# Eight single PSUM banks and one-bank FFN jobs for the first unit in a fused block-sparse attention and gated FFN kernel, under a newly written task order

## The chip, the cores and the metric

The kernel runs on one core of one Trainium2 chip. The metric is the device time of one execution in microseconds (us). The trace comes from one further, profiled execution; its span goes from the first instruction of the core to the last.

## The reference, cut to what matters

```python
# q, k, v: (4, 8, 768, 64) f32; sampled_blocks: (24, 3); blocks of 32 tokens
scores = (q @ k.T) / 8
mask = band of blocks (|i - j| <= 1) | first and last block row and column
mask |= the 3 sampled key blocks of each query block
attn = softmax(where(mask, scores, -1e9))
x = (attn @ v).transpose(0, 2, 1, 3).reshape(3072, 512)
out = (sigmoid(x @ w_gate) * (x @ w_val)) @ w_out   # 512 -> 1536 -> 512, f32 out
```

The mask is the same for all batches and heads. The kernel computes the full 768x768 scores of each head and multiplies the exponentials by the 0/1 mask (for the first unit a bias is added to the scores instead).

## The kernel before, in words

**Units.** The work is cut into 12 units: unit n is a batch b = n // 3 and 256 of its 768 queries. A unit has four pairs of heads. For a pair there are three score steps: TensorE multiplies the transposed q and k (`qT`, `kT`) into a PSUM slot of two banks, ScalarE (ACT) takes the exponential into an f16 tile `P` (L586, 128x1024), and VectorE (DVE) multiplies it by the mask (L592). In unit 0 there is no multiplication: a matmul of `bias` and `e` adds the mask to the scores. Then `value` multiplies `P` by `vex` (v with a column of ones), DVE normalises it (L655 reciprocal, L656 product) into `x`, and `x` is transposed into `xT`. For units 0 and 1, `value` uses all 128 rows of TensorE and `xT` is made by TensorE transposes (L467); for later units `value` runs as two alternating row tiles of 64, DVE folds the two halves (L646), and `xT` is made by a transposing DMA on SP's queue (L706).

**FFN.** Units 0 to 3 are FFN groups by themselves, the other eight form four groups of two. A job `f` of a group multiplies `xT` by two 128-column tiles of w_gate and w_val for one unit, or by one for two units, into a slot of two banks; ACT takes the tanh (L801) of 128x512 values, DVE makes `ht` with it (L804). Then `y` multiplies `ht` by w_out; ACT (L886) or DVE (L888) brings the result to `ysb`, and SP stores it (L878). All matmuls of scores, values and FFN are issued at one helper line, L352, so in the profile they are told apart by their tiles: `m<-qT,kT` are scores, `m<-xT,wg` FFN. TensorE is in one of two kinds of mode: whole (128 rows) or in row tiles of 64.

**PSUM.** The 16 KB of each partition are four units of two banks, `m0` to `m3`. Every task that needs PSUM takes one of the four, however little it writes, until ACT or DVE has read it.

**Inputs of batch 0.** k and q of the first pair come as f32 through SP and ACT; the other q, k, v and all weights through GpSimd (POOL) DMAs that convert to f16, in the order of `FIRST`: k1 q1 k2 q2 k3 q3 v0 v1 v2 v3 r0 w0 r1 w1 r2 w2 r3 w3 w4 w5 o0 o1 o2. Here r0 to r3 are the remaining q rows of the four pairs, w0 to w5 pairs of column blocks of w_gate and w_val, o0 to o2 w_out. q and k of batch 0 are transposed by TensorE (L467, L472) in 64-row quarters, and ACT or DVE copies them out (L297, L299). For batches 1 to 3, POOL loads a pair (L226), DVE repacks it (`pair_up`, L525, into `kp` or `qp`, one buffer for each pair), and SP issues a transposing DMA into `kT` or `qT` (L536). v is copied into `vex` by DVE (L545).

**The order.** All tasks are numbered as the program makes them. The table `ORDER` (L40 to L99) lists them in the order in which their instructions are issued. A token `123D:2@45` is task 123, on DVE, with PSUM slot 2, its load held until task 45. `Plan.run` (L137) walks through it. Each engine executes its own instructions in that order, so an instruction that waits holds up all behind it on its engine. `jN` tokens are junk matmuls that raise TensorE's clock at the start. The planner's other fields (durations, lags) are of no effect at run time.

Of the kernel before, what the change touches and what calls it, by code (L numbers as in the profile page):

```python
# [22 lines left out]
NT = S // 128  # L23
# [8 lines left out]
PE, ACT, DVE, DMA, SP = "PADGS"  # L32
# [4 lines left out]
EARLY = 2  # L37
# [3 lines left out]
j3 j3 j3 j3 j3 j3 j3 j3 5A 8D j3 0 11A j3s 9:0 j3s j3s j3s 10D j3s j3s 12:1 1:2 j3s 13A 3:0 2 j3s 34:1 4D 35 15:2  # L41
j3s 32:3 16D 6:0 33 17:1 7D 117:2 18D 97:0 118D 44:1 98A j3s 22:3 78:2 23D 45 36:0 79D 20:3 37 21D
40:2 25:1 30:3 41 26D 76:0 77D 46:1 31 54:2 19 74:0 47 75D 27:3 24 55 50:0 28D 80:1 64:3 51 81D
48:2 65 60:1 49 56:0 61 14 66:3 58:2 67D 105@30 57 29 89:3 59 38:1 90 52:0 86:2 53D 87 39 68:3
93:0 69D 62:1 108:2 94 42:3 109 43D 102:0 63D 111:3 70:1 103 110 126:2 71D 112 104 95:0 84:1 96D
122:3 85A 113 140:0 127 123 91 130:1 128 132:3 141 129 131 72:2 119:0 99:1 73D 133 120 147:2 134
100 135 142 157:0 148 154:3 171:1 124 155 149 158 88 164:3 143:2 156 176:0 92@164 144 121 146@111
101 172 170@44 165 173 161:2 217@54 145 190:1 177 189@46 162 125@40 178 237@54 159 186:3 191 150:2
115:0 151D 192 174:2 187 116 204:1 175 188 231:0 179:3 183:2 232 205 180D 244:3 184 233 206 166
245 82:0 200:2 218 83D 201 246 234:3 193:0 219 194A 152 235 185 153 211:2 136:0 220 137D 212 138  # L50
272:3 195 139 229 223A 202 167:0 255:2 168 236 273 213 221A 239 214:0 230 307:1 274 169 215 275
256 240 216 197:3 308 257 196 181 198 258 248:0 309 182 199 241:2 249 242 310 268:3 262 225:1 250
260 114@268 263 269 251 252:2 226 318:0 261 207:3 319 253 315:1 208 289:2 316 160@315 254 106:0
265:3 243 290 107A 247@265 266 270 276:1 209 291 300:0 293:3 277 301 278 282:1 294 292 283 297 163
303:0 335:2 295 302 222 304 279 227 285:1 336 296 286 238 359:0 305 337 360 210 284 331:3 228
362:1 348 332 361 264 349 363 333 328:0 287 350 329 267 322:3 351A 320 344:1 353A 311:0 323
203@344 345 341:2 387:3 321@359 312 342 317 271@282 426:1 373:0 313 411@300 427 330 397:2 374 398
343 388 346 375 259 408:1 376 389 355:2 400@268 409 390 347@30 419:0 356 334@89 380:3 405:1 428
370:2 381 306@111 364 420 288@44 406 371 386@214 366:3 421 410 365@265 454:2 422 433:1 455 432@380
# [3 lines left out]
442 474:1 484:0 463A 378 465A 339 467:2 452 340 475 524:3 480 485 525 514 354 515:1 327 468 486  # L63
# [4 lines left out]
538 583 438 550:1 567 571 542 439 586 551 638:0 563:2 572 425 539 564 552 595:1 573A 404 577:2 604  # L68
639 574 596 578 609:0 568 597 555 575A 627:2 598 616:3 610 628 617 543@616 635:1 565 712@200 630:2
611 569@300 636 612 592:3 446@563 688:0 631 593 658@60 689 654 706:1 556@231 588:3 707 579 641@550  # L70
640 642:0 632 676@471 619:1 633 589 587@282 620 594 691@214 623:2 690 613 590 670:1 591 643 671
637 605:3 624 644 621 606 645 659:1 618 625 709:0 681:3 710 626 660 607 655:2 682 692:0 656 453
663:3 711 726@99 661 657 608@234 673:2 693 662 674 622@652 664 672 694 548 699:1 695 665 723:2 666
# [3 lines left out]
762 669 782 730:3 745A 734:0 760 757:2 731 735 753 798:3 703 758 799 732 736 764:0 759 750 743A  # L77
600 765 797 826:3 823:1 767 763 824 650 816:0 766 651 827 809:1 756 768 810 719 800 787:3 817 769
733 788 806:1 801:0 807 770D 819:3 789 772A 811 737:1 790:2 839 738 614 802 580 615 791 803 601
# [5 lines left out]
904 856 925 936:0 978:1 913 937 911 857 919:3 979 908 875:0 920 914 876 929:1 921 917A 905 932  # L85
970:3 930 935 971 877 922 946:0 915A 1024:3 931 947 893 1025 928 1027:2 1012:0 939 938 916 1013
948 959:3 1028 966 1040:0 940 960 1041 1026 941 967:2 973:3 944A 942D 968 945 1029 952:0 1001:1
# [6 lines left out]
1078 1074 1094 1008 1082 1095 1083 1084 1100:1 1087A 1096A 1108:3 1088 1098A 1101 1085A 1099 1097  # L94
# [19 lines left out]

class Bank:


    def __init__(self):
        self.slot = None


class Plan:

# [13 lines left out]
    def run(self):  # L137
        done = set()
        for token in self.order:
            if token[0] == "j":  # L140
                self.idle(int(token[1]), token[2:])
                continue
# [1015 lines left out]
```

## Time and profile before

| | us |
|---|---|
| runs, as timed | 278.1, 278.46, 278.68 |
| median of the runs | 278.46 |
| the profiled execution's own time (its span) | 277.8 |
| TensorE busy | 270.0 |
| DVE busy | 207.1 |
| ACT busy | 192.1 |
| POOL (issue of DMAs) busy | 47.3 |
| granted TensorE clock | 0.999 of full |

A row of a view by windows gives the window, its length, and then for each engine the busy time and the number of instructions, the granted clock, the share of DMA engines and GB/s. A row of a timeline gives start, duration, engine, line and tiles; in brackets stands how long the engine stood idle before and what released it. The chain of waits is followed back from the last instruction: start, duration, and what the time went to. A matmul's listed duration includes the way through the pipeline; what it costs TensorE is the distance to the next start. The same holds on DVE and ACT to a smaller degree.

### The profile page before, as it was taken

How to read it: one execution, taken by the hardware profiler on the slowest of the kernel's cores; microseconds unless marked ns; L12 is line 12 of the kernel's file. 1: busy time of each engine (PE TensorE's matmuls, PEld its weight loads, DVE VectorE, ACT ScalarE, POOL GpSimd, SP SyncE). 2: the span in 40 equal slices, each digit the busy share in tenths (PEclk: the TensorE clock that was granted, in tenths of full speed). 3: DMA queues.
4: the chain of work that ended last, by engine and by line, in shares of the span. 5: the costliest groups of instructions: out<-in, count | busy, mean ns of one | idle time of the engine just before them, and what ended most of it. 6: DMA issues, size and time to landing. Idle time of an engine off the chain costs nothing.

```text
span 277.8 us, 11169 instructions
## 1 busy us (share of the span) xinstructions
PE 270.0 (97%) x5007; PEld 178.7 (64%) x5007; DVE 207.1 (75%) x421; ACT 192.1 (69%) x243; POOL 47.3 (17%) x69
## 2 busy tenths in 40 slices
PE   8879999999999999999999999999999999999995
PEld 3667785896897798655566655655655676555543
DVE  4667788899999989978988886887876899004422
ACT  3988868899989958968868965679688571035300
POOL 7776261030480000028300000000000000000000
PEclk9999999999999999999999999999999999999999
DMA  7999999994599693339986743014130002230004
GB/s 160 175 195 197 200 205 198 140 139 100 84 160 145 117 140 97 103 98 167 142 113 113 73 61 97 2 21 142 24 96 4 4 2 76 70 151 2 0 2 151
DMA packets 56684, 28.93 MB, mean 104 GB/s; under 512 B 33036, under 2 KB 53692, under 8 KB 56636
## 3 DMA queue, kind: packets, MB, share of 16 engines
q0 software_dynamic: 21520, 13.90, 35.7%
q1 hardware_dynamic: 34628, 14.02, 24.8%
q8 instruction: 39, 0.64, 1.0%
q10 hardware_dynamic: 488, 0.30, 0.3%
q14 instruction: 9, 0.07, 0.1%
HBM read 28.47 MB, written 6.29 MB: 125 GB/s over the span
## 4 chain that ended last, share of the span: by engine, by line
PE 87%; DMA 7%; POOL 2%; ACT 1%; DVE 1%; issue 1%; SPq 0%
PE m L352 86%; DMA q<-in_q_dram 3%; DMA v<-in_v_dram 2%; DMA kT<-kp 1%; ACT P L586 1%; POOL k L226 1%; POOL q L226 1%; POOL wg L236 0%; POOL wv L236 0%; DVE ysb L888 0%; DVE P L592 0%; ACT ysb L886 0%; PE m L472 0%; PE m L467 0%; ACT ysb L929 0%
## 5 line engine op out<-in xcount | busy, mean ns | idle before, releaser
L586 ACT ACTIVATE P<-m 128x1024 f16<-128x1024 f32 x144 | 143.1, 1025 | 27.8 <-PE m L352 24.6
L352 PE MATMUL m<-xT,wg 64*128 64x512 f16 (+2 forms) x720 | 136.7, 326 | 0.1
L352 PE MATMUL m<-xT,wv 64*128 64x512 f16 (+2 forms) x720 | 136.7, 326 | 0.0
L592 DVE TENSOR_TENSOR P<-P,mask 128x1024 f16<-128x1024 f16 x132 | 87.0, 684 | 2.7 <-ACT P L586 2.6
L352 PEld LDWEIGHTS <-wg 64*128 64x128 f16 (+1 forms) x720 | 66.6, 94 | 21.2 <-issue 0.8
L352 PEld LDWEIGHTS <-wv 64*128 64x128 f16 (+1 forms) x720 | 66.4, 94 | 18.2 <-issue 0.5
L804 DVE SCALAR_TENSOR_TENSOR ht<-th,m 128x512 f16<-128x512 f32 x72 | 49.0, 685 | 37.0 <-ACT th L801 36.1
L352 PE MATMUL m<-wo,ht 64*128 64x512 f16 (+2 forms) x564 | 70.4, 372 | 0.0
L801 ACT ACTIVATE th<-m 128x512 f32<-128x512 f32 x72 | 42.8, 598 | 29.6 <-PE m L352 26.1
L352 PE MATMUL m<-qT,kT 64*128 64x256 f16 x576 | 53.6, 269 | 0.9 <-DMA kT<-kp 0.5
L352 PEld LDWEIGHTS <-P 64*128 64x128 f16 (+1 forms) x2112 | 41.1, 94 | 5.2 <-issue 0.4
L352 PEld LDWEIGHTS <-ht 64*128 64x128 f16 (+1 forms) x564 | 29.4, 94 | 23.4 <-issue 1.3
L352 PE MATMUL m<-vex,P 64*128 64x65 f16 (+1 forms) x2112 | 42.5, 190 | 0.0
L352 PEld LDWEIGHTS <-kT 64*128 64x128 f16 x576 | 26.7, 94 | 17.8 <-issue 1.3
L646 DVE TENSOR_REDUCE acc<-m 128x260 f32<-128x520 f32 x40 | 27.8, 697 | 7.9 <-PE m L352 6.8
L226 POOL DMA_DIRECT2D k<-in_k_dram x15 | 11.1, 744 | 48.3 <-PE m L352 45.0
L886 ACT ACTIVATE ysb<-m 128x512 f32<-128x512 f32 x18 | 10.2, 601 | 11.8 <-PE m L352 11.8
L656 DVE TENSOR_TENSOR x<-acc,rz 128x256 f16<-128x256 f32 x40 | 17.0, 425 | 1.4
L226 POOL DMA_DIRECT2D v<-in_v_dram x16 | 11.6, 736 | 33.5 <-PE m L352 12.9
L226 POOL DMA_DIRECT2D q<-in_q_dram x19 | 13.9, 733 | 3.9 <-DMA wo<-in_moe_w_out_dram 1.8
L352 PE MATMUL m<-bias,e 64*128 64x256 f16 x48 | 5.9, 271 | 2.3 <-DVE mask L299 1.9
L929 ACT ACTIVATE ysb<-m 128x256 f32<-128x256 f32 x1 | 0.4, 383 | 10.1 <-PE m L352 10.1
(47 smaller groups left out, 84.1 us busy)
## 6 DMA issues: line engine op xcount, KB each, us to landing
out_dram<-ysb SPq DMA_DIRECT2D x23, 256.0 KB, 2.4
v<-in_v_dram POOLq DMA_DIRECT2D x16, 192.0 KB, 5.1
k<-in_k_dram POOLq DMA_DIRECT2D x15, 192.0 KB, 6.6
q<-in_q_dram POOLq DMA_DIRECT2D x12, 192.0 KB, 6.4
wg<-in_moe_w_gate_dram POOLq DMA_DIRECT2D x6, 256.0 KB, 8.4
wv<-in_moe_w_val_dram POOLq DMA_DIRECT2D x6, 256.0 KB, 9.0
wo<-in_moe_w_out_dram POOLq DMA_DIRECT2D x3, 512.0 KB, 12.8
xT<-x SPq DMA_TRANSPOSE x40, 2.4
```

Of the source, the lines that this page charges most:

```text
L226: return nc.gpsimd.dma_start(dst[:, h0:h1, t0:t1, :], src[b, h0:h1].rearrange("h (p t) d -> p h t d", t=NT)[:, :, t0:t1, :],)
L352: return nc.tensor.matmul(out, lhsT, rhs, start=start, stop=stop, skip_group_check=True).ins
L586: nc.scalar.activation(self.pt.rearrange("a h i n -> a (h i n)"), both(self.bank).rearrange("a h n -> a (h n)"), AF.Exp, bias=0.0, scale=SCALE
L592: nc.vector.tensor_tensor(self.pt, self.pt, m.unsqueeze(1).broadcast_to([128, 2, 2, UQ]), op=ALU.mult,)
L646: nc.vector.tensor_reduce(self.acc.rearrange("a h s d -> a (h s d)"), self.parts.rearrange("a r n -> a n r"), axis=mybir.AxisListType.X, o ...
L656: nc.vector.tensor_tensor(self.x16.rearrange("a s h d -> a h s d"), self.acc[:, :, :, 0:D], rz.broadcast_to([128, 2, 2, D]), op=ALU.mult,)
L801: nc.scalar.activation(th, both(bank)[:, 0, :], AF.Tanh, bias=0.0, scale=0.5)
L804: nc.vector.scalar_tensor_tensor(self.ht[:, tiles[0] : tiles[-1] + 1, :], in0=th.rearrange("a (f n) -> a f n", n=self.w), scalar=1.0, in1= ...
L886: nc.scalar.activation(ysb, both(bank)[:, s, :], AF.Copy, bias=0.0, scale=0.5)
L929: nc.scalar.activation(ysb, src, AF.Copy, bias=0.0, scale=0.5)
```

## The change: single banks, and a new order

PSUM becomes one tile `m` of eight banks. A task may take a two-bank slot (0 to 3) as before, or a single bank (a to h).

```diff
+    @property
+    def single(self):
+        return self.slot in "abcdefgh"
...
-    units_ps = [ps.tile([128, 2, 512], f32, name=f"m{i}") for i in range(4)]
+    banks = ps.tile([128, 8, 512], f32, name="m")
+    units_ps = [banks[:, 2 * i : 2 * i + 2, :] for i in range(4)]
...
+    def one(bank):
+        i = "abcdefgh".index(bank.slot)
+        return units_ps[i // 2][:, i % 2, :]
```

In a single bank a mask tile's two halves (`mask_tiles`) both use the same 64 rows and so run one after the other. Transposes go as whole 128-row transposes of 128x128, or of 128x64 for q and k, and not as four 64-row quarters. `value` of units 0 and 1 and the last outputs (`y_last`) use one bank.

```diff
-    def halves(out16, tiles):
+    def turned_in(bank, tiles):
...
+            flat = len(tile_.shape) == 2
+            if bank.single:
+                if flat:
+                    nc.tensor.transpose(one16(bank)[:, i * 128 : (i + 1) * 128], tile_, ident)
+                    continue
```

With `SMALL = 1`, unit 0's FFN is 12 jobs `f1` of one bank in place of 6 jobs `f` of two. Each has eight matmuls of 128x256, a tanh and a product of 256 columns. The first four (before: the first two) are split, so that the last quarter of the sum can come later.

```diff
-EARLY = 2
+EARLY, SMALL = 4, 1
...
+        def f1(self, f):
+
+            bank = Bank()
+            i = len(used["th1"])
+            th = home("th1", i)
...
+                                one(bank)[:, g * UQ : (g + 1) * UQ],
+                                (wg, wv)[g][:, c, f * 128 : (f + 1) * 128],
+                                self.x[:, c, :],
...
+            if self.g < SMALL:
+                for f in range(self.per * j, self.per * (j + 1)):
+                    self.f1(f)
+                return
```

The repacking `pair_up` of a pair is also made to depend on the transposing DMA that read its buffer in the batch before:

```diff
-            a = pair_up(nm, *((k16, kp) if nm == "k" else (q16, qp)), b, p, [ld] + old)
+            a = pair_up(nm, *((k16, kp) if nm == "k" else (q16, qp)), b, p, [ld] + old + turned_b.get((nm, p), []))
...
+            turned_b[nm, p] = [c]
```

`FIRST`, the tiles in SBUF, the groups and the DMAs are as they were. `ORDER` is new from the first token; TensorE's order of tasks agrees again from the second part of group 4's outputs on (161 tasks of TensorE, at about 158 us in the trace before). Its first lines:

```diff
-j3 j3 j3 j3 j3 j3 j3 j3 5A 8D j3 0 11A j3s 9:0 j3s j3s j3s 10D j3s j3s 12:1 1:2 j3s 13A 3:0 2 j3s 34:1 4D 35 15:2
+11A 8 j3 j3 j3 j3 j3 j3 j3 j3 j3 9Q:a 0 j3s 1:b 2 5 12:1 10A 3:2 4 13A j3s 34:0 6:1 7 15:3 16 82:2
```

Of its many moves, three places follow. The first is TensorE's queue where the second part of q's third pair (r2, tile `q_79`) is transposed. Before, it stands directly behind scores of unit 1:

```order
L352 MATMUL m_132<-qT_86,kT_88 128x256
L352 LDWEIGHTS kT_88
L352 MATMUL m_132<-qT_86,kT_88 128x256
L352 LDWEIGHTS kT_88
L352 MATMUL m_132<-qT_86,kT_88 128x256
L472 LDWEIGHTS q_79
L472 MATMUL m_130<-const,q_79 64x64
```

Behind the 16 transposes the first FFN job of unit 0 begins there (`m_131<-xT_159,wg`). In the changed kernel:

```order
L365 MATMUL m<-xT_156,wg 128x256
L365 LDWEIGHTS wv
L365 MATMUL m<-xT_156,wv 128x256
L365 LDWEIGHTS wg
L365 MATMUL m<-xT_156,wg 128x256
L365 LDWEIGHTS wv
L365 MATMUL m<-xT_156,wv 128x256
L501 LDWEIGHTS q_79
L501 MATMUL m<-const,q_79 64x64
```

Six of the eight matmuls of the first `f1` job now stand ahead of the transposes. So do one more score step (of unit 2) and one more pair of mask matmuls than before.

The second place is DVE's queue at the start, with the copies of v (`vex`) and of the mask out of PSUM (`CAST mask`). Before:

```order
L299 COPY kT_88<-m_130 128x2x6x64
L299 CAST mask<-m_129 128x2x256
L545 COPY vex_84<-v_83 128x12x64
L299 CAST mask<-m_129 128x2x256
L545 COPY vex_84<-v_83 128x12x64
L299 COPY qT_86<-m_132 128x2x2x64
```

In the changed kernel:

```order
L303 COPY kT_88<-m 128x2x6x64
L303 CAST mask<-m 128x2x256 x2
L303 COPY qT_86<-m 128x2x2x64
L303 CAST mask<-m 128x2x256
L580 COPY vex_84<-v_83 128x12x64 x2
L303 CAST mask<-m 128x2x256
```

The first copy of v moved behind the second to last mask tile; the copies of v now come in twos.

The third is SP's queue around the last transposing DMA of batch 2's k (`kT_88<-kp`). `xT_160` before and `xT_157` now belong to the FFN group of units 4 and 5, `out` is a store. Before, behind all eight transposes of that group:

```order
L706 DMA_TRANSPOSE xT_160<-x_153 128x2x128
L706 DMA_TRANSPOSE xT_160<-x_151 128x2x128
L706 DMA_TRANSPOSE xT_160<-x_152 128x2x128
L536 DMA_TRANSPOSE qT_86<-qp 128x6x128
L536 DMA_TRANSPOSE kT_88<-kp 128x6x128
L878 DMA out_dram<-ysb_164 128x512
```

In the changed kernel, ahead of seven of that group's eight:

```order
L740 DMA_TRANSPOSE xT_156<-x_147 128x2x128
L571 DMA_TRANSPOSE kT_88<-kp 128x6x128
L740 DMA_TRANSPOSE xT_157<-x_150 128x2x128
L740 DMA_TRANSPOSE xT_157<-x_145 128x2x128
L965 DMA out_dram<-ysb_159 128x512
L740 DMA_TRANSPOSE xT_157<-x_146 128x2x128
```

The transposition of k is now issued ahead of seven transposes that stood before it, and of the stores among them.

More of the change, by code (lines that the diff above doesn't have):

```diff
@@ L31 @@
 NU = S // UQ
-PE, ACT, DVE, DMA, SP = "PADGS"
+PE, ACT, DVE, DMA, SP, ONE = "PADGSQ"
 VB = 5
@@ L429 @@
         ),
[L430 removed]
+        [(DVE, 0.335)],
     )
     t_rows = [
[L433 removed]
+        rows(S, lambda eng, spread: copy(eng, mb24, spread), [(DVE, 0.87), (ACT, 0.70)])
     ]
@@ L438, in mask_tiles, with half @@
         bank = Bank()
+        w = c1 - c0
+        def half(i):
+            return one(bank)[:, i * w : (i + 1) * w] if bank.single else both(bank)[:, i, 0:w]
         def mm(eng):
@@ L498, in turn @@
                 tiles = [pr[:, t, :] for t in range(t0, t1)]
-            halves(both16(bank), tiles)
+            turned_in(bank, tiles)
         def evac(eng):
@@ L664, in turn @@
             x16 = self.x16.rearrange("a s h d -> a s (h d)")
-            halves(both16(self.bank2), [x16[:, s, :] for s in range(2)])
+            turned_in(self.bank2, [x16[:, s, :] for s in range(2)])
         def evac(self, eng):
@@ L748, in scores @@
             take=run[0][1].bank,
-            ops=16 if first else 8,
+            score=True,
+            needs=("e0", "e1") if first else (),
         )
@@ L835, in f @@
                     take=bank,
-                    ops=16 * self.per,
-                    wide=True,
+                    mode="W",
+                    needs=wneeds,
                 )
@@ L844, in f @@
                     take=bank,
-                    lag=GAP,
-                    ops=16 * self.per,
+                    needs=wneeds,
                 )
                 a = plan.add(
-                    [(PE, F_HALF)], half(False), [a], ops=16 * self.per
+                    [(PE, 0.863 if self.w == 512 else 0.872)], half(False), [a], turn=True
                 )
             used["xT"][self.g].append(a)
-            c = plan.add([(ACT, 0.57)], tanh, [a] + before("th", i), free=bank, part=1)
-            g = plan.add([(DVE, 0.68)], gate, [c], free=bank, part=1)
+            old = before("th", i)
+            if i < len(rings["th"]) and used["th1"]:
+                old = [x for m in (2 * i, 2 * i + 1) for x in used["th1"][max(k for k in used["th1"] if k % 6 == m)]]
+            c = plan.add([(ACT, 0.477)], tanh, [a] + old, free=bank)
+            g = plan.add([(DVE, 0.598)], gate, [c], free=bank)
             used["th"][i] = [g]
@@ L898, in part @@
                     take=bank if first and f0 == 0 else None,
-                    lag=0.0 if f0 < 8 else GAP if first else None,
-                    ops=16,
+                    turn=not first and f0 == 0,
+                    needs=(f"o{f0 // 4}",),
                 )
```

315 lines of the change are left out of this document (177 added, 138 removed), and 49 rows, old and new, of the table ORDER.

## The prediction

> **What bounds the kernel now.** I begin with the view by cores and windows (time, length, then busy us and instructions of TensorE, its weight loads, DVE, ACT, POOL).
>
> ```profile
> core 0: 277.8 us, clock 0.999
> ```
>
> ```profile
> 14.00:21.00 7.00, 5.64 (x142) 4.49 (x145) 4.51 (x13) 5.67 (x6) 5.04 (x8) 1.00 1.44 195
> 21.00:28.00 7.00, 6.42 (x135) 5.07 (x136) 5.37 (x15) 6.14 (x8) 4.81 (x7) 1.00 1.45 197
> 28.00:35.00 7.00, 7.00 (x86) 5.20 (x85) 5.29 (x11) 5.58 (x7) 1.48 (x3) 1.00 1.38 200
> 62.00:127.00 65.00, 64.47 (x1512) 49.19 (x1510) 58.99 (x120) 55.41 (x67) 12.14 (x17) 1.00 0.69 117
> ```
>
> The clock is full, and from 28 us on TensorE is never idle for long. So TensorE's own work bounds the kernel, and a new order can gain only what TensorE waits for. The view of waits lists that, longest first (us in all, times, longest):
>
> ```profile
> PE m L352 <- DVE mask L299: 1.9, 1, 1.9
> PE m L329 <- DVE junk L206: 1.0, 1, 1.0
> PE m L352 <- DMA kT<-kp: 0.5, 1, 0.5
> PE m L352 <- DVE x L656: 0.3, 1, 0.3
> PE m L472 <- DMA q<-in_q_dram: 0.2, 1, 0.2
> ```
>
> The 1.9 us are the largest, but the chain of waits says that they are not on the path that sets the end:
>
> ```profile
> 15.57 8.08 DMA q<-in_q_dram
> 23.69 0.32 PE m L472 x16
> ...
> 25.64 0.30 DVE xT L299
> ...
> 118.66 4.07 DMA kT<-kp
> 122.73 0.05 issue
> 122.78 82.12 PE m L352 x1516
> 204.90 0.02 issue
> 204.92 0.60 ACT ysb L886
> 205.53 0.02 issue
> 205.55 0.70 DVE ysb L888
> 206.25 0.04 issue
> 206.30 68.39 PE m L352 x884
> ```
>
> At 23.69 TensorE is let go by the load of r2, the late rows of q's third pair, which landed 8.08 us after its issue. Had the mask come earlier, TensorE would have waited for r2 the longer. Behind 23.69 the chain is TensorE itself, but for the copy of `xT` at 25.64, `kT` at 118.66, and the `ysb` copies at 204.92. These three places are what this order loses after the start.
>
> **The change part by part.**
>
> *Start: r2 stays, more work goes ahead of it.* The order of POOL's loads is unchanged, and each waits on loads, not on TensorE:
>
> ```profile
> 14.61 0.74 POOL L236 DMA_DIRECT2D wv<-in_moe_w_val_dram  x1 [0.28 <-DMA v<-in_v_dram]
> 15.57 0.70 POOL L226 DMA_DIRECT2D q<-in_q_dram  x1 [0.22 <-issue]
> ...
> 23.27 0.74 POOL L236 DMA_DIRECT2D wv<-in_moe_w_val_dram  x1 [0.66 <-DMA wv<-in_moe_w_val_dram]
> ```
>
> So r2 lands at 23.65 again, and the transposes of `q_79` start at 23.69 at the earliest. All that counts is how much work now stands ahead of them that came after them before. The prices are the distances of starts in TensorE's timeline:
>
> ```profile
> 22.85 0.61 PE L352 MATMUL m<-qT,kT 64*128 64x256 f16 x8 [0.29 <-DVE x L656]
> 23.69 0.32 PE L472 MATMUL m<-const,q 64*64 64x64 f16 x16 [0.23 <-DMA q<-in_q_dram]
> ...
> 24.06 0.27 PE L352 MATMUL m<-xT,wv 128*128 128x256 f16 x1
> 24.17 0.27 PE L352 MATMUL m<-xT,wg 128*128 128x256 f16 x1
> ...
> 28.68 0.27 PE L352 MATMUL m<-xT,wv 128*128 128x256 f16 x1
> 28.89 0.32 PE L472 MATMUL m<-const,q 64*64 64x64 f16 x16
> ```
>
> A 128x256 matmul costs 0.11 (24.06 to 24.17), so the six of the first `f1` job cost 0.66. The score step of unit 2 costs 0.22: two steps, eight matmuls, are listed with 0.61, of which the last one's way through the pipeline is 0.16 (0.27 less the distance of 0.11), and half of the remaining 0.45 is one step. The extra pair of mask matmuls costs as much, 0.22, since in one bank its halves run in turn. Sum 1.10 us moved ahead. Against it: that `f1` job needs the second block of w_val. The POOL issue at 23.27 waited for just that landing, so it landed about 0.28 earlier, at 22.99. Then 0.66 of matmuls, and 0.1 for the change from whole to tiled mode (28.68 to 28.89 is 0.21, against 0.11 between equals) bring the transposes to about 23.80, 0.11 later than before. Net **-1.0**. The bounds: 0, if the work ahead is itself late, and -1.3, since the 0.23 that TensorE stood idle there can be filled too.
>
> The 1.9 us wait had this origin on DVE:
>
> ```profile
> 14.35 0.36 DVE L545 COPY vex<-v 128x768 f16<-128x768 f16 x1 [1.53 <-DMA v<-in_v_dram]
> 14.63 0.68 DVE L299 CAST mask<-m 128x512 f16<-128x512 f32 x1
> ```
>
> DVE stood 1.53 us for v with a mask tile queued behind the copy. Now the copies of v stand behind seven of eight mask tiles, so this wait goes; it is what gives TensorE the time to do the 1.10 us of work ahead of r2. It is no saving of its own.
>
> *The wait for kT.* The 0.5 us wait at 122.78 is for the transposition of batch 2's last k, issued at 118.66 behind all eight `xT` transposes of units 4 and 5. In the new order it stands ahead of seven of them. From the timeline of SP:
>
> ```profile
> 112.26 5.01 SPq L706 DMA_TRANSPOSE xT<-x  x3
> ...
> 117.37 1.24 SPq L536 DMA_TRANSPOSE qT<-qp  x1
> ...
> 118.66 1.29 SPq L536 DMA_TRANSPOSE kT<-kp  x1
> ```
>
> One xT transpose takes a slot of 1.2 to 1.7 us there, so seven give it over 8 us of lead against a lateness of 0.5. Added up, TensorE's starts fall 0.7 behind the sum of their usual distances at this place, 0.5 for the wait and the rest for the restart: **-0.7**, bounds 0 to -0.7.
>
> *The wait for ysb.* At 206.30 TensorE waits for a bank that DVE empties only after ACT did the other half, with 1.21 us of idleness on DVE:
>
> ```profile
> 205.55 0.69 DVE L888 TENSOR_SCALAR ysb<-m 128x512 f32<-128x512 f32 x1 [1.21 <-ACT ysb L886]
> ```
>
> In the new order the DVE half stands first and waits for TensorE alone. **-0.3** (the idle time before 206.30 in the weight loads is 0.29), bounds 0 to -0.3.
>
> *Waits between 24 and 40 us.* The wait for `xT` at 25.98 (copied at 25.64, 0.30) costs 0.2 and goes, since other work stands between. But 12 one-bank jobs bring 12 tanh and 12 products in place of six and six, and new work on TensorE runs nearer to ACT and DVE there: the score steps behind the q transposes need the copy of them by DVE first. Price **-0.2 + 0.5**; the 0.5 is an estimate by the nearest waits, 0.3 and 0.2 in the list above; its bounds are 0 and 1.2 (four such waits).
>
> *Changed matmuls.* Masks in one bank cost their halves in turn, eight of nine pairs by 0.11 each more, that is 0.9; whole 128-row transposes 0.8, an estimate at 0.05 each (half of a 256-wide matmul) against 0.02 for a quarter (0.25 for 16 from 28.89 on); fewer junk matmuls take 0.45 off. Most of this lies ahead of r2 and is paid in waiting time. Behind r2 TensorE's work is equal: 0; if the part ahead of r2 were paid in full, it would cost up to 0.5 more, which is within the bound of 0 for the start's gain.
>
> *DVE from 62 to 127 us.* The order of that stretch is packed anew. The window row above has DVE busy for 58.99 of 65 us before. Counted by order, over the same TensorE work, DVE gets 51 mask products for 46, 15 gates for 16, 30 value parts for 29, and 20 copies of k, q and v for 15. By these rows
>
> ```profile
> 206.16 2.49 DVE L592 TENSOR_TENSOR P<-P,mask 128x1024 f16<-128x1024 f16 x4
> ```
>
> ```profile
> L545 DVE COPY vex<-v 128x768 f16<-128x768 f16 x16 | 5.7, 354 | 1.5 <-DMA v<-in_v_dram 1.5
> ```
>
> a product costs 0.6 in a row (2.49 for four, the last one longer), and a copy 0.27 to 0.35. The difference is 3.0 - 0.6 + 0.6 + 1.5 = 4.5 us, so 63.5 of 65 us, 98 per cent. An average of that kind hides lateness: the products are for later units and may slip, but any wait of DVE for ACT or TensorE is now paid. I take **+0.6**, near the single waits of 0.3 to 0.7 that this order had; bounds 0 and 2.
>
> Together: -1.0 - 0.7 - 0.3 - 0.2 + 0.5 + 0.6 = -1.1. The profiled execution's own time was 277.8, 0.66 below the median of 278.46. I take the difference off the median, which is the metric: 278.46 - 1.1 = **277.4 us**.
>
> **The rivals.**
>
> *Slower: DVE becomes the bound from 62 to 127 us.* Only 1.5 us of slack are left there. If each of DVE's some 125 instructions is late by 0.02 us on average (semaphores, a neighbour's wait), 2.5 us come up, 1.0 more than the slack; with the waits for ACT that before cost DVE (2.6 us in eight over the kernel) that makes 2 to 2.5 more instead of 0.6, while the gains at the start stay at their low end. 278.46 - 1.1 + 1.9 = 279.3. It decides from the point at which DVE's lateness exceeds the slack of 1.5. For it: 98 per cent. Against it: much of the work is early.
>
> *Late loads.* Eleven of the loads of batches 1 and 2 are issued in one burst and copied by DVE soon after:
>
> ```profile
> 72.33 2.16 POOL L226 DMA_DIRECT2D k<-in_k_dram  x3
> ```
>
> Their copies now come earlier in DVE's queue. A copy that waits holds up all of DVE, and TensorE then lacks masked `P`. One such wait cost 1.53 at 14.35; half of that, 0.8, makes 278.1.
> This row gives 0.72 us for one issue, while DVE is 91 per cent busy. The Trainium skill, "SBUF — State Buffer", section "Who interferes with whom", says that copies in VectorE's two-port mode lock out GpSimd, whose DMA descriptors then come late; by that, 5 more copies of 0.35 would delay the issues by up to 1.8 us. The trace has no sign of a longer issue so far.
>
> *No change.* The work ahead of r2 is late by itself, since it needs `x`, masks and banks, and the start brings only -0.2; the rest nets -0.1: 278.2.
>
> *All waits go* and nothing new comes: -1.3 - 0.7 - 0.3 - 0.2 = -2.5, that is 276.0.
>
> **How the numbers follow.** A measurement of this kernel tells 0.2 per cent, 0.56 us, from no change: faster is below 277.90, slower above 279.02. The forecast (276.8 to 277.9) has 0.45, all waits gone 0.13, no change or late loads 0.20, DVE as the bound or another new wait 0.22. Faster 0.58, same 0.20, slower 0.22. The range of 276.2 to 279.3 leaves out some 0.08 below and 0.12 above.
>
> **What would show it.** Right: TensorE has no wait for a mask copy near 15 us; the transposes of `q_79` start at 23.7 to 23.9 right behind six FFN matmuls; no waits for `kT<-kp` and none for `ysb` at 206. Wrong: r2 lands at another time; waits of TensorE for `P` of DVE in the windows from 62 to 127, with DVE at 98 per cent there; a DVE copy that waits for a k, q or v load; waits for banks between 24 and 40 us above 0.5 in sum. From about 158 us on the rest should take as long as before; if it doesn't, the cause is not in this sum.

## The result, and the profile after

The changed kernel takes 285.54 to 290.81 us in four runs, against 278.57 (median) for the kernel before on the same chip. The ratio is 1.0261, with an interval from 1.0219 to 1.0303. On a second chip it took 287.83 (four runs from 287.01 to 289.16) against 278.72, a ratio of 1.0332 (1.0277 to 1.0387). So it is 7 to 9 us slower, where 1.1 us of gain was forecast, outside the range of 276.2 to 279.3.

Two executions of the changed kernel were profiled. They show the same two causes in different shares. The first (290.81 us as timed) is one of two runs in a slower state, which the ratio leaves out, so sizes are taken from the second (287.83) where that is possible.

**The start gained as much as was forecast, but not in the way that was forecast.** TensorE's timeline of the changed kernel, first execution, at the transposes of r2 (`q_79`):

```profile
23.39 0.27 PE L365 MATMUL m<-xT,wv 128*128 128x256 f16 x1
23.59 0.32 PE L501 MATMUL m<-const,q 64*64 64x64 f16 x16
```

They start at 23.59, behind six matmuls of the first `f1` job, while 23.69 was the time before and 23.80 the forecast. To see what that is worth I again add up the usual distances of TensorE's starts. At 50 us the changed kernel has 220.9 us of such work left, the kernel before has 221.9. It is 1.0 us ahead of that one execution.

But r2 did not hold the transposes back any more. POOL issued its load at 14.47, not at 15.57:

```profile
14.47 0.70 POOL L230 DMA_DIRECT2D q<-in_q_dram  x1 [0.30 <-DMA v<-in_v_dram]
```

It landed 8.3 us later, at 22.76 (22.93 in the second execution), where 23.65 was forecast. The transposes started behind TensorE's own work. The time of that landing differs from one execution to the next, with the old order too. Two experiments below run the old order with nothing changed before 93 us. In their traces r2 lands at 22.06 and 22.47, and the wait for the mask is 0.6 and not 1.9. These rows are of the second of them, with the two moves:

```profile
22.92 0.32 PE L469 MATMUL m<-const,q 64*64 64x64 f16 x16
```

```profile
PE m L349 <- DVE mask L296: 0.6, 1, 0.6
```

Its transposes start at 22.92, those of the other at 22.79. With the 1.10 us of work that the new order puts ahead of them they would start at 23.9 to 24.0. The new order has them at 23.59, so against these two traces it gains 0.3 to 0.4. Most of the 1.0 is how late r2 was in the one profile that the forecast was read from.

The wait for `kT` and that for `ysb` at 206 are gone as well. In the list of TensorE's waits of the first execution (us in all, times, longest) neither stands. The first three rows:

```profile
PE m L365 <- DVE ht L904: 4.9, 3, 2.3
PE m L365 <- issue: 2.1, 2, 1.8
PE m L365 <- DVE acc L681: 1.2, 1, 1.2
```

What stands there instead is 8 us of new waits, all between 50 and 125 us. In the second execution another row leads the list:

```profile
PE m L365 <- issue: 5.0, 5, 2.0
```

The row by windows for 62 to 127 us, which the forecast of DVE rested on, first execution and then second:

```profile
62.00:127.00 65.00, 59.30 (x1375) 51.18 (x1373) 54.11 (x112) 50.60 (x63) 15.04 (x21) 0.96 1.17 142
```

```profile
62.00:127.00 65.00, 59.38 (x1358) 49.39 (x1356) 55.35 (x115) 52.54 (x64) 15.76 (x22) 0.97 1.15 144
```

TensorE was busy for 64.47 of these 65 us and is now for 59.3. DVE isn't full: it was busy for 58.99 and is now for 54 to 55. What has risen is the share of the DMA engines, from 0.69 to 1.15. (It goes above 1, so I read it as a measure of crowding only.) POOL issues 21 or 22 loads here where it issued 17. The view of DMA from 45 to 127 us gives the packets of POOL's queue (q0) and of SP's (q1), and the median us from issue to landing. Before, and then the changed kernel's second execution:

```profile
q1 hardware_dynamic: 18416, 6.03, 41.6%
q0 software_dynamic: 5388, 3.90, 35.0%
...
v<-in_v_dram POOLq DMA_DIRECT2D x9, 192.0 KB, 4.8
...
kT<-kp SPq DMA_TRANSPOSE x8, 3.6
```

```profile
q0 software_dynamic: 8591, 6.21, 63.1%
q1 hardware_dynamic: 19872, 6.17, 53.7%
...
v<-in_v_dram POOLq DMA_DIRECT2D x12, 192.0 KB, 5.8
...
kT<-kp SPq DMA_TRANSPOSE x9, 6.3
```

The new order brings loads of batches 2 and 3 forward: the first load of batch 2 goes out at 49.5 us in the second execution and at 72.3 before, the first of batch 3 at 70.9 and at 123.5 before. Half as much again is loaded in these 82 us, and a transposition takes 6.3 us to land where it took 3.6.

**First cause: DVE stands in front of copies.** The chain of waits of the first execution, its middle part:

```profile
48.70 11.00 DMA q<-in_q_dram x2
...
59.72 0.36 DVE qp L560
60.08 0.61 DVE ht L904
...
60.73 4.62 PE m L365 x85
...
80.09 10.34 DMA v<-in_v_dram
...
90.46 0.36 DVE vex L580
90.82 0.61 DVE ht L904
...
91.47 20.16 PE m L365 x451
```

The chain goes from a load to DVE's copy of it, from there to the product `ht` behind the copy, and from `ht` to TensorE. DVE's timeline has the idle time ahead of those copies in brackets:

```profile
54.23 0.36 DVE L560 COPY qp<-q 128x768 f16<-128x768 f16 x1 [1.15 <-DMA q<-in_q_dram]
59.72 0.36 DVE L560 COPY qp<-q 128x768 f16<-128x768 f16 x1 [2.18 <-DMA q<-in_q_dram]
77.65 0.36 DVE L560 COPY qp<-q 128x768 f16<-128x768 f16 x1 [1.58 <-DMA q<-in_q_dram]
90.46 0.36 DVE L580 COPY vex<-v 128x768 f16<-128x768 f16 x1 [4.73 <-DMA v<-in_v_dram]
```

Nobody needs these copies yet. By the tasks' order and TensorE's timeline, the first task that uses them starts at 73.3, 107.7, 119.2 and 132.1 us. What is held up is the work behind them. In the second execution such waits of DVE are shorter (3.2 for v, 1.2 for q, in all) and cost TensorE only 0.7. That copies by themselves can cost several us is seen below, in the run with plain DMAs.

**Second cause: TensorE runs out of instructions.** A wait `<- issue` is one for which the profile shows no releaser. In the chain of the second execution such waits stand alone between TensorE's own work:

```profile
67.71 1.00 issue
68.71 6.64 PE m L365 x112
75.36 0.61 issue
75.97 5.59 PE m L365 x128
81.56 1.98 issue
83.54 6.94 PE m L365 x128
```

128 matmuls with their 128 weight loads are 256 instructions. The page's part on DMA queues has a queue that carries them (packets, MB, share of 16 engines):

```profile
q8 instruction: 39, 0.64, 1.0%
```

These are 39 packets of 16 KB, and TensorE has 39 times 255 instructions. Counted over TensorE's program, every such stop lies at instruction 194 + 256n, in the middle of a task. So a packet is a page of 256 instructions, and it is fetched about when the page ahead of it starts. From the packets' times and the starts of those instructions I worked out the following for the second execution (us; the wait in the queue is counted from the start of the page ahead):

```
page ahead starts   packet runs      waited in queue   page starts   stop
      61.46        66.36 -  67.29         4.89            68.71      1.38
      68.71        73.30 -  74.44         4.59            75.97      0.80
      75.97        81.38 -  82.34         5.41            83.54      2.25
     100.81       104.40 - 106.48         3.59           107.96      1.51
     117.23       121.08 - 122.00         3.84           123.43      1.08
kernel before, the pages nearest to these:
      60.81        62.53 -  63.74         1.71            67.29      0.00
      81.99        83.84 -  84.90         1.86            87.77      0.00
     112.00       112.66 - 114.30         0.66           119.58      0.02
```

By this count the packet waits 3.6 to 5.4 us in the DMA engines' queues, runs for about 1 (once 2.1), and the page starts 1.2 to 1.5 us after. The page ahead kept TensorE at work for 5.1 to 6.5 us, so the next one comes too late. In the kernel before, the wait in the queue from 50 us on is at most 2.6, and no page is late.

Added up for the second execution, TensorE falls 10.9 us behind its usual distances from 50 to 125 us: 7.4 at page starts, 1.7 by a lower clock after the stop of 1.98, 0.7 by the copy at 57.70, and the rest in small pieces. Before, it fell 1.5 behind there, 0.7 of it for `kT`. In the first execution it is 13.9 us: 7.0 by DVE's copies, 2.9 at page starts, 3.0 by a lower clock.

### The profile page after: what moved, and what is told of

Read it like the earlier page. It is cut to its first block, busy times and chain, and to the rows that moved or that the text cites. A ratio compares the mean times of both kernels' runs of the same rounds, so it can differ in the third digit from the quotient of the medians.

```text
span 289.0 us, 11103 instructions
## 1 busy us (share of the span) xinstructions
PE 276.0 (95%) x4969; PEld 187.4 (65%) x4969; DVE 208.0 (72%) x429; ACT 190.8 (66%) x247; POOL 47.2 (16%) x69
## 4 chain that ended last, share of the span: by engine, by line
PE 69%; DMA 20%; issue 5%; POOL 4%; DVE 1%; ACT 0%; POOLq 0%
PE m L365 69%; DMA q<-in_q_dram 6%; DMA wo<-in_moe_w_out_dram 5%; DMA v<-in_v_dram 4%; DMA wg<-in_moe_w_gate_dram 3%; DMA wv<-in_moe_w_val_dram 3%; POOL q L230 1%; POOL k L230 1%; POOL v L230 1%; DVE ht L904 0%; POOL wg L240 0%; DVE qp L560 0%; DVE acc L681 0%; ACT ysb L1015 0%; DVE e L211 0%
## 5 line engine op out<-in xcount | busy, mean ns | idle before, releaser
L365 PE MATMUL m<-xT,wv 64*128 64x512 f16 (+2 forms) x720 | 139.0, 330 | 6.5 <-DVE ht L904 4.4
L365 PE MATMUL m<-xT,wg 64*128 64x512 f16 (+2 forms) x720 | 138.5, 329 | 0.0
L904 DVE SCALAR_TENSOR_TENSOR ht<-th,m 128x512 f16<-128x512 f32 x66 | 44.7, 684 | 31.4 <-ACT th L901 30.9
L901 ACT ACTIVATE th<-m 128x512 f32<-128x512 f32 x66 | 39.3, 599 | 29.3 <-PE m L365 22.9
L365 PEld LDWEIGHTS <-ht 64*128 64x128 f16 (+1 forms) x564 | 31.1, 94 | 25.0 <-issue 1.7
L365 PEld LDWEIGHTS <-P 64*128 64x128 f16 (+1 forms) x2112 | 42.8, 96 | 6.3 <-issue 2.6
L365 PE MATMUL m<-vex,P 64*128 64x65 f16 (+1 forms) x2112 | 44.4, 192 | 1.7 <-DVE acc L681 1.2
L365 PEld LDWEIGHTS <-kT 64*128 64x128 f16 x576 | 29.9, 94 | 14.1 <-issue 1.8
L580 DVE COPY vex<-v 128x768 f16<-128x768 f16 x16 | 5.8, 373 | 4.7 <-DMA v<-in_v_dram 4.7
L560 DVE COPY qp<-q 128x768 f16<-128x768 f16 x12 | 4.3, 354 | 4.9 <-DMA q<-in_q_dram 4.9
```

Of the source, the lines that this page charges most:

```text
L365: return nc.tensor.matmul(out, lhsT, rhs, start=start, stop=stop, skip_group_check=True).ins
L560: nc.vector.tensor_copy(dst[:, p, :, :, :], src[:, 2 * p : 2 * p + 2, :, :].rearrange("a h t d -> a t h d"),)
L580: nc.vector.tensor_copy(vex[b % 2][:, 2 * p : 2 * p + 2, :, 0:D], v16[:, 2 * p : 2 * p + 2, :, :],)
L901: nc.scalar.activation(th, both(bank)[:, 0, :], AF.Tanh, bias=0.0, scale=0.5)
L904: nc.vector.scalar_tensor_tensor(self.ht[:, tiles[0] : tiles[-1] + 1, :], in0=th.rearrange("a (f n) -> a f n", n=self.w), scalar=1.0, in1= ...
```

## The experiments

Lines of kernels with a changed order stand a few numbers lower than in the changed kernel. The theories, which the expectations name by letters where they need to: first, that loads land late because the transposing DMAs (in particular) run at the same time (A), against the rival that the loads' time is as before and only the place of the copies in DVE's queue counts; then, for the stops with no releaser, that late pages of instructions make them (E), against something else in the new order (F).

**The changed kernel again, as it is.**

> The changed kernel once more, without an edit, beside the runs of before on this chip. Theory A (loads and transposing DMAs get in each other's way, and VectorE's copies wait for the loads): 283 to 290 us, with VectorE waiting some 9 us in all for loads of q and v. Theory B (VectorE has too much work from 62 to 127 us): the same time, but without long waits of VectorE for loads in an undisturbed run.

Measured: 287.83, ratio 1.0332 (1.0277 to 1.0387). It is the second execution of the lists above. The time is within the expectation, but DVE waited 5.6 us in all for loads of k, q and v, where some 9 were expected for q and v. The copies cost 0.7 here and the pages most of the rest, so copies alone don't explain the loss.

**Four copies later in DVE's queue.** Each of the four copies of the timeline above moves behind other copies, still well ahead of its first use.

```diff
-253 293 282 294 295
+278 249 282 385@251 97:3
-382:0 383 318 271 384
+260 346 318 305:0 306
-299 407:2 359 364:3
+430 279 359 420@361
-446:2 378 395 396
+440 444 378 441 442
```

> Four copies of VectorE that waited for a load (q of batch 1's last pair, q of batch 2's first and second pair, v of batch 2's second pair) stand later in the order, by 2 to 15 us; each is first used later still. No work is taken away. Theory A: the waits of 1.2, 2.2, 1.6 and 4.7 us go, TensorE's waits behind them too, and the time falls to 276.5 to 280 us. Theory B (VectorE is full): the same work in the same stretch, so over 283 us. Theory C (the loads come too late for TensorE itself, wherever the copy stands): TensorE waits for transposed k or q instead, over 283 us.

Measured: 284.04 (282.85 to 285.37), 1.0191 (1.0142 to 1.0240), on the chip of the run above: 3.8 us less. TensorE's wait for `ht` is gone from its list; this stays:

```profile
PE m L362 <- issue: 3.7, 4, 1.3
```

These are page starts at 61.60, 69.13, 76.11 and 82.58, with packets that waited 3.80 and 5.25 us in the queue for the first two. The time missed the expectation of 276.5 to 280. Nor were the 3.8 us gained mainly at the copies: of the 5.0 us between the two profiled executions (spans of 286.1 and 281.1) the copy's 0.7 is a small part. The stops at pages fell from 7.4 to some 4.6 by the distances, and the 1.7 by the lower clock is gone. So this run doesn't show by itself what the copies cost.

**All transposing DMAs as plain ones.**

```diff
-            nc.sync.dma_start_transpose(
+            nc.sync.dma_start(
```

> All transposing DMAs on SP's queue (k and q of batches 1 to 3, x of units 2 to 11) are replaced by plain DMAs of the same bytes between the same tiles, so what is computed is not the reference; the order and all waits stay. Theory A: the loads take 4 to 6 us from issue to landing in place of 7 to 10, VectorE's waits for them shrink below 1 us in all, and the time is 275 to 279 us. Theory C (the loads are issued too late, whatever else runs) and theory D (VectorE's copies hold up the issue of the loads): the loads take as long as in the changed kernel, and the time stays over 283 us.

Measured: 283.16 (281.69 to 285.56), 1.0167 (1.0103 to 1.0230): 4.7 us less, and still over the 275 to 279 that were expected. From 45 to 127 us TensorE has no stop at a page start above 0.1 us. The packets of SP's queue from 45 to 127 us fell from 19872 to 5760 for the same bytes, and their share of the engines' time from 53.7% to 22.5%:

```profile
q1 hardware_dynamic: 5760, 6.16, 22.5%
```

But DVE still waits for loads, and TensorE for DVE:

```profile
PE m L365 <- DVE ht L904: 4.2, 3, 2.4
```

```profile
DVE vex L580 <- DMA v<-in_v_dram: 2.9, 1, 2.9
DVE qp L560 <- DMA q<-in_q_dram: 2.2, 1, 2.2
```

So it isn't transposition in particular that makes loads late, and that part of the theory falls: the median load lands only 0.4 to 1.2 us earlier than in the second execution (v 5.4, q 4.5, k 5.5). Without late pages TensorE waits 4.2 us for products that stand behind copies. That is what the copies cost in that run, with the clock at 1.00. What SP's queue asks of the engines does show in the pages. Whether the number of its packets or their kind makes the difference isn't separated here.

**Loads, transposing DMAs and plain DMAs, alone and together.** A kernel of DMAs only, five stages: four loads, eight transposing DMAs, both, eight plain DMAs, plain DMAs with loads.

> Only DMAs, nothing of the computation: four loads of a pair alone (POOL's queue), eight transposing DMAs of 128x768 alone (SP's queue), both at once, eight plain DMAs of the same size on SP's queue alone, and these at once with the four loads. Theory A: alone, the loads land after 3.5 to 7 us and the transposes need 1.3 us each; at once, the loads land after 7 to 12 us, or the transposes stretch from some 12 us to over 15; with plain DMAs at once the loads land within 8 us. Theories B, C and D: loads and transposes at once take what each takes alone, within 1 us.

The time of a stage is read from the trace's DMAs, from the first issue to the last landing. Loads alone: issued from 4.96 on, landed at 8.50, 10.51, 12.04 and 13.02, 8.1 us. Transposing DMAs alone: 13.22 to 25.39, 12.2 us. Both together: 25.60 to 40.27, 14.7 us, with the loads landing 4.9 to 7.1 after their issue where it was 3.5 to 5.8 alone. Plain ones alone: 6.7 us, and 13.4 with the loads (47.38 to 60.78), whose landings then come 4.5 to 10.4 after the issue, where theory A had them within 8. Both kinds of DMA share engines with the loads: with plain ones the times nearly add up (6.7 + 8.1 against 13.4), with transposing ones a part overlaps.

**Both edits: later copies and plain DMAs.**

> The four late copies and the plain DMAs in place of the transposing ones together (what is computed is not the reference). Theory E (two costs add up: VectorE's copies that wait for loads, and TensorE's own instructions, which come in pages of 256 through the same DMA engines and are late when these are full): each of the two edits alone left about 4.9 us of waits of TensorE in its trace, of the other kind; together under 1.5 us, 276.5 to 279.5 us. Theory B (VectorE is full): over 281 us, as each alone.

Measured: 281.65 (279.00 to 283.88, ten runs), 1.0080 (1.0043 to 1.0117) against 278.39. The median misses the expectation by 2 us and falls where theory B had it (over 281); one run of the ten is inside the expectation. In the profiled run, with 279.73, TensorE's new waits are 0.6 for DVE and 0.5 at a page, the next ones 0.3: no sign there of a full DVE. The two edits bring the ratio from 1.033 to 1.008. What keeps the other runs 2 us above the profiled one isn't shown.

**Batch 3's loads and copies moved back; and batch 2's too.** Two orders on top of the later copies, to thin the traffic. One of the moves of batch 3, a transposing DMA (569), and one of a load (563), that both have:

```diff
-577:1 689 569 578 656
+590 528 569 690:3
-415 300 563@414 325 250
+374 583:2 563@583 584 542
```

> The late copies, and besides the twelve loads of batch 3 (with the copies and two transposes that hang on them) are put back to the time from 110 to 135 us, where they were before; batch 2's loads stay early. Theory E: instruction pages of TensorE are no longer late from 70 to 125 us, but the stops at 61 and 69 us stay; 280 to 283 us. If the stops are no matter of the DMA engines: the same 284 us as with the late copies alone.

> As the run with batch 3's loads late, and the first four loads of batch 2 are held until batch 1's transposes are through, at about 62 us, with their copies later. The order of TensorE's and ScalarE's work is that of the changed kernel. Theory E: no stop of TensorE at a page of instructions over 0.5 us, no long wait of VectorE for a load, 276.5 to 278.5 us, that is below before. Theory B: over 281 us.

Both missed: 291.33 (1.0422, interval 1.0365 to 1.0478) and 289.96 (1.0394, 1.0346 to 1.0442). My moves made a wait of their own. The transposing DMAs of batch 3 now stood on SP's queue ahead of transposes of `x` that TensorE needs at 130 us:

```profile
PE m L362 <- DMA xT<-x: 5.9, 2, 5.6
```

```profile
PE m L362 <- DMA xT<-x: 6.8, 1, 6.8
PE m L362 <- issue: 3.1, 3, 2.0
```

The stops at pages fell to 1.7 in the first, and stayed at 3.1 in the second, at 73, 81 and 87 us; that the loads of batch 2 meet the transposes there isn't shown.

**Pages by themselves.** A kernel of bare matmuls: 1024 of 65 columns alone, 1024 of them beside 8 loads and 8 transposing DMAs, 384 of 512 columns beside the same DMAs.

> Nothing of the computation: 1024 small matmuls of 65 columns in two row tiles alone, the same beside eight loads and eight transposing DMAs, 384 matmuls of 512 columns beside the same DMAs, and the DMAs alone. Theory E: alone, 256 instructions (128 matmuls with their weight loads) take at least 2.3 us, the time that a page needs, though 48 such matmuls took 0.73 us (1.9 us for 128) in the kernel; beside the DMAs a page takes 4 to 8 us; the large matmuls (some 14 us for a page) run without stops beside the same DMAs. If instructions don't come through the DMA engines: the small matmuls take the same with and without DMAs.

TensorE's timeline of the first stage, without any DMA, and of the second:

```profile
10.11 2.12 PE L241 MATMUL m<-P 64*128 64x65 f16 x128 [0.24 <-issue]
13.56 2.12 PE L241 MATMUL m<-P 64*128 64x65 f16 x128 [1.34 <-issue]
17.02 2.12 PE L241 MATMUL m<-P 64*128 64x65 f16 x128 [1.34 <-issue]
```

```profile
44.32 3.71 PE L241 MATMUL m<-P 64*128 64x65 f16 x128 [6.82 <-issue]
51.07 3.70 PE L241 MATMUL m<-P 64*128 64x65 f16 x128 [3.04 <-issue]
```

Alone, a page of 128 short matmuls takes 2.12 us and the next follows after 3.45: TensorE stops 1.34 for each page even with idle DMA engines. With several pages fetched ahead the first full stop would not come as early as the third page, as it does. Beside DMAs the stops are 3.04 and 6.82. The matmuls of 512 columns ran from 70.69 to 112.3 without a stop beside the same DMAs, where a page lasts 13.8 us.

The Trainium skill, "Runtime: NRT & Kernel Launch", section "Instruction fetch mechanics", says that an engine refills its instruction memory in blocks of 16 KiB, 256 instructions, by a DMA queue of its own, and that the cost of crossing a block is mostly hidden. The trace agrees on block and queue (39 packets, 0.64 MB). The cost is hidden in the kernel before (at most 0.02 us at the pages of the table above). It isn't here, with 1.34 us for each block, nor in the changed kernel, with up to 2.25.

**The kernel before, with spare DMAs.** Eleven DMAs for which nobody waits, from SBUF to a buffer in DRAM, are spread over 93 to 116 us of the kernel before.

```diff
+    spare = nc.dram_tensor("spare", (11, 128, S), f32, kind="Internal").ap()
+    for i in range(11):
+        plan.add(
+            [(DMA, 0.72)],
+            lambda eng, i=i: nc.gpsimd.dma_start(spare[i], e64),
+        )
```

> The kernel before, word for word, plus eleven DMAs on POOL's queue between 93 and 112 us, each writing a constant tile to a spare tensor in DRAM that nothing reads or waits for (beside the full computation). Theory E: TensorE stops for 0.5 to 3 us at starts of its pages of 256 instructions between 95 and 125 us, with no instruction or transfer named as what it waits for; the time grows by 3 to 10 us. Theory F (a full DMA queue hurts only through the data that are waited for): waits named for the transposed k, q or x alone, none at page starts.

Measured: 283.45 (282.94 to 284.54), 1.0170 (1.0132 to 1.0207). TensorE's new stops are all at page starts; these rows are of its timeline:

```profile
102.92 0.28 PE L350 MATMUL m<-xT,wv 64*128 64x256 f16 x1 [0.46 <-issue]
...
108.66 0.27 PE L350 MATMUL m<-xT,wg 64*128 64x256 f16 x1 [0.47 <-issue]
...
114.84 0.24 PE L350 MATMUL m<-vex,P 64*128 64x65 f16 x4 [1.93 <-issue]
```

The packets of these pages waited 2.91, 3.19 and 3.79 us, the stops are 0.73, 0.74 and 2.13 by the distances. The order of TensorE, DVE and ACT is that of before. So DMA traffic alone, which no instruction waits for, makes pages late, and these eleven DMAs of 384 KB cost 4.8 us in the kernel before: theory E is shown, and F isn't needed for the stops. It is not the price of the changed kernel's own traffic, which is of another size and kind. POOL's queue got few packets more here (6529 for 5388 from 45 to 127 us), but its share of the engines' time rose from 35.0% to 53.6%.

**The kernel before, with two moves.** Its transposing DMA of the late `kT` ahead of two stores, and DVE's half of `ysb` ahead of ACT's.

```diff
-530:2 464 545 503
-653 497 466 557:3
+425 464 466 539
-973:3 944A 942D 968
+973:3 942D 944A 968
```

> The kernel before with two moves in its order: two output stores of SP's queue go behind the transposition of batch 2's last k, and the half of ysb that VectorE empties at 205 us goes ahead of ScalarE's half. By the prediction's terms the wait of 0.7 us at 122.8 and that of 0.3 us at 206.3 go: 277.3 to 277.9 us where before has 278.4. If other work is late right behind these waits: 278.2 to 278.6 us.

Measured: 279.01 (277.93 to 280.46, twelve runs), 1.0014 (0.9989 to 1.0038). Neither 277.3 to 277.9 nor 278.2 to 278.6, the two expectations, was met. The wait for `kT` is gone from the list of waits, and still no gain can be told: the runs of the kernel before on that chip go from 277.81 to 280.56.

**Loads and transposes in turns.** The reference's whole work, the later copies, and batch 2's and 3's loads and transposing DMAs moved so that the ones are issued while the others are few, without the jam at 130 us.

> The changed kernel with its loads and its transposing DMAs in turns: late copies, batch 2's first loads held to 62 us, batch 2's transposes held until the x transposes of about 90 us, batch 3's loads from 115 us on, and batch 3's first transpose behind the x transposes of unit 5, which had held up TensorE by 6 to 7 us in the two runs before. TensorE's and ScalarE's order is that of the changed kernel. Theory E: page stops below 1 us in all from 45 to 125 us, and 276.5 to 279.5 us. If the order of TensorE's work itself costs time: over 281 us with no stop at pages.

Measured: 281.33 (279.95 to 281.64), 1.0083 (1.0052 to 1.0113), 5 to 7 us less than the changed kernel by the two ratios. The time misses theory E's 276.5 to 279.5 and falls where the rival had it: over 281 without stops at pages, if the order of TensorE's work itself costs time. The trace speaks against that rival, since TensorE has less work left at 50 us than in the profile before, by the usual distances, and what it loses from there to 125 us is mostly waits with a name. That the rival has no part in the last 2 us isn't shown. The largest stop at a page is 0.42; the landings are again near those of before (`kT` 4.3, v 4.9). What stays above all is one copy, and its effect on TensorE:

```profile
73.26 0.36 DVE L557 COPY kp<-k 128x768 f16<-128x768 f16 x1 [1.50 <-DMA k<-in_k_dram]
```

```profile
PE m L362 <- DVE acc L678: 1.1, 1, 1.1
```

It is still slower than the kernel before. No version that I ran has a median below that of the kernel before.

## Why the prediction was wrong, point by point

*What bounds the kernel.* TensorE's own work did bound the kernel before. The conclusion that a new order "can gain only what TensorE waits for" says what can be gained, not what can be lost, and the sum had a loss in one term only, DVE's.

*The start, -1.0, and the waits from 24 to 40 us, -0.2 + 0.5.* Together -0.7 was forecast, and -1.0 was measured at 50 us against the same profile. The number is near, the mechanism isn't what was forecast, and the agreement is in part luck. The work moved ahead as forecast, six matmuls among it. But "r2 lands at 23.65 again" failed, by the prediction's own list of signs: it landed at 22.76 and 22.93, and the transposes waited for TensorE's own work. Against the two other traces of the old order the gain is 0.3 to 0.4.

*The median that the sum starts from.* The prediction set the profiled span of 277.8 against the median of 278.46 and took the profiled execution for a little faster than the median. A span and a time as run aren't the same measure: the runs with both on record are timed 1.7 to 1.8 us above their span. So 277.8 belongs to some 279.6 as timed, an execution 1.1 us slower than the median. The waits read from it, the late r2 above all, could not be taken off the median in full.

*The wait for kT, -0.7, and for ysb, -0.3.* Both are gone in the trace of the changed kernel. The gain can't be told in the time of the changed kernel, and the two moves done alone on the kernel before gave 1.0014, not 0.9964: it isn't shown that they are worth 1.0 us.

*DVE from 62 to 127 us, +0.6, and the rival "DVE becomes the bound".* The count of 63.5 of 65 us assumed that TensorE does the same work in that time. It didn't: DVE was busy for 54 to 55 us, since it stood in front of copies and TensorE in front of pages. This rival falls; in the version with loads and transposes in turns, DVE does reach 60.86 there, without a loss of this kind.

*The failed step: the late loads.* Its mechanism is one of the two that were found: "a copy that waits holds up all of DVE". It stood among the rivals and not in the sum, and its size was set by one wait of the start, halved, 0.8 us, as if one copy would wait once. The change moved at least four copies far ahead of their use, and the loads themselves landed later (2.18 and 4.73 us of idleness in the first execution, 3.25 for the v copy in the second, instead of 1.53). In the run with plain DMAs TensorE waits 4.2 us behind copies; in the changed kernel itself it is 7.0 in the first execution and 0.7 in the second. Doing four copies later took 3.8 us off the changed kernel, by the two traces mostly through fewer stops at pages and no lower clock.

*The missing step: the price of the DMA traffic itself.* The prediction gave the DMA engines no term: it put their price at nothing, without a reason. It counted five more copies in that stretch, but not that their loads and transposing DMAs have to pass the same engines in the same 82 us, and that TensorE's instructions pass there too. In the second execution the late pages cost 7.4 us, and 1.7 more by the lower clock. The spare DMAs show that traffic alone can do this (4.8 us for eleven of them); plain DMAs in place of the transposing ones took 4.7 off the changed kernel. With both causes eased the ratio falls from 1.033 to 1.008.

The rule of the Trainium skill, "SBUF — State Buffer", section "Who interferes with whom", that the prediction weighed, is not borne out as far as the trace shows: one issue on POOL takes 0.71 to 0.73 us all through the stretch where loads are late, and the six that run beside a copy of DVE there (second execution) take no longer than the others.

*What stays open.* How much of the 9 us belongs to each cause can't be split cleanly, since a stop of TensorE shifts the loads and a late load shifts the pages; the two profiled executions show 7.0 against 2.9, and 0.7 against 7.4. What the last 2 us of the eased versions consist of is only partly read (the copy at 73.26, which costs 1.1, and small waits). A program of the same work with fewer instructions for TensorE, whose pages would last longer, wasn't tried.

## What to carry to other kernels

Before an order that moves loads forward is priced, add up the time of the DMAs that it puts into each stretch, and compare with the share of the DMA engines there. Neither bytes nor packets alone tell it: the plain DMAs moved the same bytes without late pages, and the spare DMAs made pages late with few packets. A dense stretch of short matmuls needs its next page of 256 instructions from the same engines in the time that the page ahead lasts, 5.1 to 6.5 us for the late pages here. A copy of a loaded tile belongs as late in its engine's queue as its first use allows, since everything behind it waits for the load. A wait `<- issue` in the middle of a task, at distances of 256 instructions, is a late page.

## What the runs showed of the hardware

TensorE has about one page of instructions ahead of it: with idle DMA engines, and matmuls that last 2.12 us for a page, one page took 3.45 us from start to start. In that trace the packet of the next page ran from 11.16 to 12.19 where pages started at 10.11 and 13.56: about 1 us until it runs, 1 us for it, and 1.4 until the page starts. A stop of about 2 us can cost a second time by the clock. The rows by windows for the changed kernel's second execution, after the stop at 81.56, and for the next stretch:

```profile
83.50:90.40 6.90, 6.86 (x128) 6.25 (x128) 4.07 (x8) 3.68 (x5) 0.45 (x1) 0.75 1.40 174
90.50:100.00 9.50, 9.45 (x248) 7.91 (x248) 9.20 (x22) 8.14 (x10) 2.86 (x4) 1.00 0.56 76
```

The granted clock was 0.75 in the mean of 6.9 us, which is 1.7 us lost. After the stop of 1.93 with spare DMAs it was 0.72 over 6.2 us. The wait of 1.9 near 15 us in the kernel before was not followed by this: the clock was 1.00 from 15.3 to 20.
